# Rows of x stored from GpSimd's queue instead of SyncE's, and expert 0's first weights requested two iterations earlier

## The chip, the cores and the metric

One core of one Trainium2 chip runs the whole program. Its engines are TensorE (PE, with its weight loads shown as PEld), VectorE (DVE), ScalarE (ACT), GpSimd (POOL) and SyncE (SP); here SP only issues transfers. The metric is the device time of one execution in microseconds (us); lower is better.

## The reference, cut to what matters

Local attention over chunks of 64 positions is followed by a mixture of eight experts, all in fp32. B=8, S=576, eight heads of 64, F=1024.

```python
scores = scale * q_c @ k_c.T                  # per chunk of 64, scale = 1/8
attn = softmax(scores);  x = attn @ v_c       # x: [B, S, 512] after the heads are joined
for b in range(B):
    prev_e = -1
    for s in range(S):
        fresh_e = argmax(x[b, s] @ w_gate)
        e = fresh_e if s == 0 or sigmoid(x[b, s] @ w_local) < 0.5 else prev_e
        prev_e = e
        out[b, s] = softmax(x[b, s] @ w_gate)[e] * (relu(x[b, s] @ w1[e]) @ w2[e])
```

## The kernel before, in words

**Attention.** The 4608 rows are cut into 18 units of 256 rows. `place` maps a unit to its rows: sixteen units are 256 neighbouring rows of one batch; units 4 and 13 are leftover units, made of the last 64 rows of each of four batches. A unit goes through these steps: `load_qk` and `load_v` bring q, k and v in; `a_pair` (`pair_heads`, line 174) has POOL copy q and k into the buffers `qr` and `kr`, two copies each; `a_tq` transposes these on PE, and ACT moves the result out of PSUM; `a_sa` makes scores and their softmax; `a_tp` transposes the probabilities; `a_va` makes the values and writes normalised rows to `xs`; `a_tx` transposes these; `a_ra` (`router`) makes the gate's logits, copies them beside the rows (line 320, `xs<-L`) and stores rows and logits in the DRAM tile `x_d`. An `xs` tile is 128 partitions of two rows of 528 floats, 528 KB in all.

**Software pipeline.** Fifteen iterations of the loop at line 848 play the order `PAR["steady"]`, each working on several units at once: iteration i loads q and k of unit i+5 and v of unit i+2, runs scores of unit i+1, probabilities of unit i, values of unit i-1, transposes of q and k of unit i+2, and router and store of unit i-2, and at its end the POOL copies of unit i+3. The `qr` and `kr` buffers exist once, so these copies wait until PE has read the ones before. q and k have three load buffers each, v three, `xs` four. Order on PE, ACT, DVE and POOL is the order of the program (`manual_schedule`); every queue works in order, so an instruction that waits holds what is behind it.

**Weights of expert 0.** `load_w1(0, c)` requests a quarter of the first weight matrix (512 KB) into `raw1[c]`, after iterations 6, 8, 10 and 12. After iterations 8 to 15 `split` turns half a quarter into a high part (ACT, line 105, `w1h`) and a low part (POOL, line 106, `w1l`): quarter c is split after iterations 8+2c and 9+2c.

**Routing and experts.** `PAR["hooks"]` places the routing of the first nine units (`route`, `slots`) into iterations 10 to 15: small chains over DVE and PE, one-hot rows `rh` on DVE and POOL (line 464, in iteration 14), and `early_gather`, three indirect transfers on POOL's queue that read `x_d` (line 673). After the loop `PAR["drain"]` finishes the last four units beside the first expert tiles; then tiles of 128 rows go through their experts, with gathers and scatters on POOL's queue.

**Queues.** SP issues every plain transfer: q, k, v, weights, and the rows of x. POOL issues only the indirect ones.

Of the kernel before, what the change touches and what calls it, by code (L numbers as in the profile page):

```python
# [20 lines left out]
B, H, S, D = 8, 8, 576, 64  # L21
# [3 lines left out]
P = 128  # L25
# [49 lines left out]
def tile_attention_then_moe(ctx: ExitStack, tc, q, k, v, wg, wl, w1, w2, out):  # L75
    nc = tc.nc
# [5 lines left out]
    x_d = dpool.tile([N, XR], F32, name="x_d")  # L82
# [15 lines left out]
    def load_w1(e, c):  # L98
        nc.sync.dma_start(raw1[c], w1[e, P * c:P * c + P, :])

    def load_w2(e, c):
        nc.sync.dma_start(raw2[c], w2[e, 256 * c:256 * c + 256, :].rearrange("(f p) d -> p f d", p=P))

    def split(hi, lo, raw, lo_eng=None):
        nc.scalar.copy(hi, raw)
        (lo_eng or nc.vector).tensor_tensor(lo, raw, hi.bitcast(F32), ALU.subtract)
# [20 lines left out]
    def place(i):  # L127
        ph, j = divmod(i, 9)
        if j == LEFT:
            return 9 * ph + 8, [(4 * ph + n, 512, 64) for n in range(4)]  # L130
        j -= j > LEFT
        return 9 * ph + j, [(4 * ph + j // 2, 256 * (j % 2), 256)]
# [163 lines left out]
    def router(i, xT, xs, fine=False):  # L296
        lg = ps_l.tile([P, 2, 256], F32, name="lg")
        lT = pa2.tile([P, LW], F32, name="lT", bufs=1)[:, 0:256]

        def mm():  # L300
            for c in range(4):
                nc.tensor.matmul(lg[32 * c:32 * c + 32, 0], wg9[:, c], xT[:, c], start=True, stop=True)
            if not fine:
                cp()

        def cp():
            nc.vector.tensor_copy(lT, lg[:, 0])

        def tr():
            for cc in range(2):  # L310
                nc.tensor.transpose(lg[:, 1, P * cc:P * cc + P], lT[:, P * cc:P * cc + P], ident)
            if not fine:
                red()

        def red():
            slot, rows = place(i)
            Lt = L[:, 2 * slot:2 * slot + 2, :]
            nc.vector.tensor_reduce(
                Lt, lg[:, 1].rearrange("p (t c e) -> p t e c", t=2, c=4)[:, :, 0:9, :], AX.X, ALU.add)
            nc.vector.tensor_copy(xs[:, :, C:XL], Lt)  # L320
            if len(rows) == 1:
                (b, s0, n), = rows
                nc.sync.dma_start(x_d[S * b + s0:S * b + s0 + n, :].rearrange("(c p) n -> p c n", p=P), xs)
            else:
                for m, (b, s0, n) in enumerate(rows):
                    nc.sync.dma_start(x_d[S * b + s0:S * b + s0 + n, :], xs[64 * (m // 2):64 * (m // 2) + 64, m % 2])

        return [mm, cp, tr, red] if fine else [mm, tr]

    def ok(i):  # L330
        return 0 <= i < NS
# [140 lines left out]
    def a_tq(i, engs=None):  # L472
        qkT[i] = (pe2.tile([P, 4, 256], F32, name="qT", bufs=1), pe2.tile([P, 4, 256], F32, name="kT", bufs=1))
        return qk_transposes(hd.pop(i), *qkT[i], engs)

    def a_pair(i, engs=(nc.gpsimd,) * 4):
        hd[i], fns = pair_heads(qk.pop(i), engs)
        return fns

    def a_sa(i, fine=False):  # L480
        prs[i] = pa2.tile([P, H, 2, D], F32, name="pr")
        return scores(*qkT.pop(i), prs[i], fine)

    def a_tp(i, fine=False):
        pTs[i] = pa2.tile([P, H, P], F32, name="pT")
        return p_transposes(prs.pop(i), pTs[i], fine)

    rows = []

    def a_va(i, fine=False):  # L490
        if not rows:
            rows.extend(pa2.tile([P, XS], F32, name=f"xs{n}", bufs=1) for n in range(NX))
        xss[i] = rows[i % NX][:, 0:2 * XR].rearrange("p (c n) -> p c n", c=2)
        if i < NX:
            nc.gpsimd.memset(xss[i][:, :, XL:XR], 0.0)
        return values(pTs.pop(i), vts.pop(i), xss[i], fine)

    def a_tx(i, fine=False):
        xTs[i] = pa2.tile([P, 4, 256], F32, name="xT", bufs=1)
        return x_transposes(xss[i], xTs[i], fine)  # L500

    def a_ra(i, fine=False):
        return router(i, xTs.pop(i), xss.pop(i), fine)

    def play(order, qs):
        its = {}
        for tok in order.split():
            name, _, n = tok.partition("*")
            if name not in its:
                its[name] = iter(qs[name]())  # L510
            for _ in range(int(n or 1)):
                next(its[name])()
        for name, it in its.items():
            assert next(it, None) is None, name
        assert set(its) == set(qs), set(qs) - set(its)

    def run(fns):
        for fn in fns:
            fn()
# [54 lines left out]
    with tc.manual_schedule(engines=MAN | {ET.Pool}):  # L574
# [3 lines left out]
        def load(store, fn, i):  # L578
            def go():
                store[i] = fn(i)  # L580
            return lambda: [go]
# [266 lines left out]
    for i in range(1, NS - 2):  # L848
        qs4 = dict(s=lambda: a_sa(i + 1), tp=lambda: a_tp(i), va=lambda: a_va(i - 1, True), tq=lambda: a_tq(i + 2))
        opt = dict(lq=load(qk, load_qk, i + 5) if ok(i + 5) else None,  # L850
                   lv=load(vts, load_v, i + 2) if ok(i + 2) else None,
                   pr=(lambda: a_pair(i + 3)) if ok(i + 3) else None, tx=(lambda: a_tx(i - 2)) if i >= 2 else None, ra=(lambda: a_ra(i - 2, True)) if i >= 2 else None)
        for h in range(4):
            opt[f"h{h}"] = (lambda h=h: [lambda: run(hooks[i, h])]) if (i, h) in hooks else None
        toks = [t for t in PAR["steady"].split() if opt.get(t.split("*")[0], 1) is not None]
        play(" ".join(toks), qs4 | {k: v for k, v in opt.items() if v is not None})
        if i in (6, 8, 10, 12):
            load_w1(0, i // 2 - 3)
        if 8 <= i < 16:
            c, col = divmod(i - 8, 2)  # L860
            col = slice(512 * col, 512 * col + 512)
            split(w1h[c][:, col], w1l[c][:, col], raw1[c][:, col], nc.gpsimd)
# [9 lines left out]
    n = NS - 1  # L872
# [27 lines left out]
    def gather_full(t):  # L900
        xgs[t] = gather(t, pc.tile([P, XR], F32, name="xg", bufs=4), x_d)
# [27 lines left out]
        s=lambda: sa, ld=lambda: [lambda: [load_w2(0, c) for c in (2, 3)]], rt=lambda: sb, rk=sb_rank, of=lambda: offsets, oh=sb_onehots,  # L929
        sl=lambda: slots([pc, pc, pc], QB[1], QB[2], ((0, NT),), qs), ex=lambda: experts,  # L930
        g=lambda: [lambda t=t: gather_full(t) for t in (EARLY, EARLY + 1)],
# [294 lines left out]
```

## Time and profile before

| | |
|---|---|
| time, median of 3 runs | 650.72 us (648.82 to 650.81) |
| profiled execution, its own time | 656.88 us |
| its span, first to last instruction | 655.1 us |
| mean granted clock of TensorE over the span | 0.991 |
| PE busy | 616.1 us, 94% of the span |
| DVE, ACT, POOL busy | 378.2, 258.2, 147.2 us |
| attention with its router | about the first 172 us |

Times inside the trace count from the start of the span. In the rows, an arrow from the right ("out<-in") names what an instruction writes and reads, "xN" counts instructions merged in one row, and square brackets hold the idle time of the engine just before the row and what ended it. A row "SPq" is SP issuing a transfer; its length is the time that SP needed to hand it over, not the time to its landing. A busy PE is not PE at its peak.

### The profile page before, as it was taken

The numbers are of one execution on the slowest core, as the hardware profiler recorded it, in microseconds if no ns is written. First come the engines' busy times: TensorE is split into PE (matmuls) and PEld (weight loads), VectorE is DVE, ScalarE is ACT, GpSimd is POOL, SyncE is SP. The second block draws the span as 40 slices with busy tenths as digits, with TensorE's granted clock in tenths as the row PEclk, the third lists the DMA queues.
The fourth block names the chain that finished last, engine by engine and source line by source line (L and its number), as shares of the span: only waits on it lengthen the run. The fifth ranks groups of instructions, "written<-read, shape, count | busy, mean of one in ns | idle before, by whom it ended". The sixth has DMA issues, their size and how long they took to land. (4 is left out here: it accounts for less than half of the span.)

```text
span 655.1 us, 17357 instructions
## 1 busy us (share of the span) xinstructions
PE 616.1 (94%) x5904; PEld 517.2 (79%) x5904; DVE 378.2 (58%) x983; ACT 258.2 (39%) x469; POOL 147.2 (22%) x217
## 2 busy tenths in 40 slices
PE   4799997989999999999999999999998999999995
PEld 4678886766788788788899996789887988788883
DVE  2567676987784767475433465763477533377231
ACT  4567785756412153531212433531464211343130
POOL 4423343550050112022021021022011212010201
PEclk9999998999999999999999999999998999999998
DMA  8999899989622054055121065451075511154201
GB/s 241 237 275 292 229 267 288 294 218 310 197 77 94 35 181 170 28 179 175 39 68 52 22 212 157 146 173 56 33 246 209 189 53 49 37 180 134 82 21 37
DMA packets 102521, 97.90 MB, mean 149 GB/s; under 512 B 42256, under 2 KB 79120, under 8 KB 102352
## 3 DMA queue, kind: packets, MB, share of 16 engines
q1 hardware_dynamic: 96192, 75.82, 38.7%
q0 software_dynamic: 6160, 19.99, 9.3%
q8 instruction: 86, 1.41, 0.9%
q14 instruction: 83, 0.68, 0.4%
HBM read 76.62 MB, written 19.69 MB: 147 GB/s over the span
## 5 line engine op out<-in xcount | busy, mean ns | idle before, releaser
L783 POOL DMA_INDIRECT out<-ysb,sidx x38 | 40.9, 1076 | 364.4 <-DVEq L979 163.2
L722 PE MATMUL y<-w2h,hq 128*128 128x512 f32 x368 | 119.4, 395 | 1.2 <-ACTq L1001 1.0
L1014 PEld LDWEIGHTS tr<-xp,w1h 128*128 128x128 f32 x704 | 87.7, 191 | 4.0 <-ACT w2h L963 1.5
L1014 PE MATMUL tr<-xp,w1h 128*128 128x256 f32 x704 | 90.2, 283 | 0.7 <-ACTq L979 0.5
L722 PEld LDWEIGHTS y<-w2h,hq 128*128 128x128 f32 x368 | 69.3, 189 | 16.7 <-issue 2.1
L722 PE MATMUL y<-w2l,hq 128*128 128x512 f32 x184 | 72.2, 393 | 2.5 <-DVE w2l L969 1.5
L1022 ACT ACTIVATE hq<-tr 128x256 fp32r<-128x256 f32 x68 | 25.2, 383 | 107.4 <-PE tr L1014 60.9
L722 PE MATMUL y<-w2h,hp 128*128 128x512 f32 x192 | 63.1, 396 | 0.5 <-ACT hp L669 0.3
L701 PE MATMUL h<-w1h,xp 128*128 128x512 f32 x208 | 60.8, 398 | 0.0
L1023 DVE SCALAR_TENSOR_TENSOR hq<-tr,hq 128x256 fp32r<-128x256 f32 x68 | 28.1, 424 | 38.7 <-ACT hq L1022 36.8
L1014 PE MATMUL tr<-xp,w1l 128*128 128x256 f32 x352 | 47.6, 283 | 0.0
L1014 PEld LDWEIGHTS tr<-xp,w1l 128*128 128x128 f32 x352 | 44.6, 192 | 0.0
L701 PEld LDWEIGHTS h<-w1h,xp 128*128 128x128 f32 x208 | 37.8, 188 | 7.6 <-ACTq L979 0.4
L722 PEld LDWEIGHTS y<-w2l,hq 128*128 128x128 f32 x184 | 34.8, 189 | 10.2 <-DVE w2l L969 2.4
L673 POOL DMA_INDIRECT xg<-x_d,gidx x36 | 38.3, 1064 | 19.5 <-issue 13.3
L722 PEld LDWEIGHTS y<-w2h,hp 128*128 128x128 f32 x192 | 36.0, 188 | 8.3 <-DVE hp L670 0.6
L768 ACT ACTIVATE hsb<-h 128x512 f32<-128x512 f32 x26 | 14.1, 596 | 65.6 <-PE h L701 49.4
L969 DVE TENSOR_TENSOR w1l<-raw,w1h 128x1024 fp32r<-128x1024 f32 x28 | 32.4, 1220 | 12.1 <-ACT w1h L963 10.6
L722 PE MATMUL y<-w2l,hp 128*128 128x512 f32 x96 | 37.6, 392 | 0.5 <-DVE w2l L969 0.5
L1043 DVE TENSOR_SCALAR ysb<-y,ppr 128x512 f32<-128x512 f32 x32 | 24.0, 751 | 23.5 <-PE y L722 22.5
L969 DVE TENSOR_TENSOR w2l<-raw,w2h 128x1024 fp32r<-128x1024 f32 x28 | 32.8, 1221 | 5.2 <-ACT w2h L963 3.2
L963 ACT CAST w2h<-raw 128x1024 fp32r<-128x1024 f32 x28 | 28.0, 1046 | 13.8 <-PE m L734 3.8
(229 smaller groups left out, 1062.3 us busy)
## 6 DMA issues: line engine op xcount, KB each, us to landing
raw<-in_moe_w SPq DMA_DIRECT2D x72, 512.0 KB
x_d<-xs SPq DMA_DIRECT2D x16, 528.0 KB
qt<-in_q SPq DMA_DIRECT2D x15, 512.0 KB
kt<-in_k SPq DMA_DIRECT2D x15, 512.0 KB
v<-in_v SPq DMA_DIRECT2D x20, 256.0 KB
raw<-in_v SPq DMA_DIRECT2D x12, 256.0 KB
x_d<-xs SPq DMA_DIRECT2D x8, 132.0 KB
qt<-in_q SPq DMA_DIRECT2D x8, 128.0 KB
```

The source lines that it names most:

```text
L673: nc.gpsimd.indirect_dma_start(out=dst, out_offset=None, in_=src, in_offset=bass.IndirectOffsetOnAxis(ap=gidx[t].bitcast(U32), axis=0))
L701: nc.tensor.matmul(hs[:, j], xs[a][:, c], W1[w][c][:, 512 * j:512 * j + 512], start=(c == 0 and n == 0), stop=(c == 3 and n == 2))
L722: nc.tensor.matmul(y, h_of(t, f // 4)[a][:, f % 4], W2[w][c][:, f % 2, :], start=(f == 0 and n == 0), stop=(f == 7 and n == 2))
L768: nc.scalar.activation(hsb[:, 512 * j:512 * j + 512], hs[:, j], AF.Relu)
L783: nc.gpsimd.indirect_dma_start(out=out, out_offset=bass.IndirectOffsetOnAxis(ap=sidx[t].bitcast(U32), axis=0), in_=ysb, in_offset=None, bo ...
L963: nc.scalar.copy(hi[c], raw[c])
L969: V.tensor_tensor(lo[c], raw[c], hi[c].bitcast(F32), ALU.subtract)
L1014: nc.tensor.matmul(hb[:, 256 * n:256 * n + 256], W1[w][c][:, P * (f + n):P * (f + n) + P], XP[:, x, c].rearrange("p s t -> p (s t)"), star ...
L1022: nc.scalar.activation(hi, ps, AF.Relu)
L1023: V.scalar_tensor_tensor(lo, ps, 0.0, hi.bitcast(F32), ALU.max, ALU.subtract)
L1043: V.tensor_scalar(ysb, y, pr, None, ALU.mult)
```

## The change

The rows of a unit go to `x_d` from POOL's queue, with the same shape as before for an ordinary unit; a leftover unit's four stores of 64 rows become two of 128 rows. The requests for expert 0's first weights move from the end of iterations 6, 8, 10, 12 to the end of 4, 6, 8, 10; their splits stay.

```diff
             nc.vector.tensor_copy(xs[:, :, C:XL], Lt)
+            xv = x_d.rearrange("(b s) n -> b s n", s=S)
             if len(rows) == 1:
                 (b, s0, n), = rows
-                nc.sync.dma_start(x_d[S * b + s0:S * b + s0 + n, :].rearrange("(c p) n -> p c n", p=P), xs)
+                nc.gpsimd.dma_start(xv[b, s0:s0 + n].rearrange("(c p) n -> p c n", p=P), xs)
             else:
-                for m, (b, s0, n) in enumerate(rows):
-                    nc.sync.dma_start(x_d[S * b + s0:S * b + s0 + n, :], xs[64 * (m // 2):64 * (m // 2) + 64, m % 2])
+                for g in range(2):
+                    b, s0, n = rows[2 * g]
+                    nc.gpsimd.dma_start(xv[b:b + 2, s0:s0 + n].rearrange("c p n -> p c n"), xs[64 * g:64 * g + 64])
...
-        if i in (6, 8, 10, 12):
-            load_w1(0, i // 2 - 3)
+        if i in (4, 6, 8, 10):
+            load_w1(0, i // 2 - 2)
```

## Rows read from the trace of the kernel before

**Rows 1.** Windows: stretch, length, busy us (count) per engine, clock, DMA share, GB/s.

```profile
60.50:67.80 7.30, 7.30 (x173) 5.95 (x172) 5.24 (x15) 5.48 (x10) 2.34 (x4) 1.00 1.07 287
...
75.00:82.20 7.20, 7.20 (x171) 5.94 (x170) 5.13 (x14) 5.39 (x10) 2.34 (x4) 1.00 0.71 197
96.80:109.70 12.90, 9.50 (x178) 7.49 (x176) 8.06 (x27) 7.50 (x14) 4.27 (x7) 0.87 1.04 292
...
134.50:143.20 8.70, 7.92 (x189) 6.57 (x188) 6.73 (x24) 5.57 (x10) 4.03 (x5) 1.00 0.57 166
...
200.00:420.00 220.00, 217.09 (x1318) 185.74 (x1316) 124.81 (x309) 69.81 (x134) 34.78 (x33) 1.00 0.34 111
```

**Rows 2.** Timeline of SP's queue, 64 to 144 us, some of its rows.

```profile
64.94 1.84 SPq L323 DMA_DIRECT2D x_d<-xs  x1
...
73.49 4.88 SPq L326 DMA_DIRECT2D x_d<-xs  x4
78.41 0.58 SPq L99 DMA_DIRECT2D raw<-in_moe_w  x1
...
95.03 0.46 SPq L99 DMA_DIRECT2D raw<-in_moe_w  x1
...
102.91 1.32 SPq L323 DMA_DIRECT2D x_d<-xs  x1
...
115.12 5.03 SPq L154 DMA_DIRECT2D v<-in_v  x4
...
134.96 2.31 SPq L323 DMA_DIRECT2D x_d<-xs  x1
143.07 1.62 SPq L154 DMA_DIRECT2D v<-in_v  x2
```

**Rows 3.** Timeline, all engines, around the split of the second quarter.

```profile
101.47 0.62 ACT L105 CAST w1h<-raw 128x512 fp32r<-128x512 f32 x1 [2.91 <-DMA raw<-in_moe_w]
...
102.72 0.63 PE L182 MATMUL tr<-ident,qr 128*128 128x128 f32 x4 [2.46 <-ACT xT L172]
...
109.35 0.49 PE L388 MATMUL tr<-ident,sc 18*1 18x18 f32 x4 [0.84 <-DVE sc L381]
```

**Rows 4.** Windows of 5 us around that wait, columns as in rows 1.

```profile
45.00:50.00 5.00, 3.42 (x86) 2.82 (x80) 2.62 (x6) 2.48 (x5) 0.00 (x0) 1.00 1.02 309
...
100.00:105.00 5.00, 2.54 (x21) 1.68 (x20) 3.00 (x7) 2.90 (x6) 2.44 (x3) 0.89 1.05 283
105.00:110.00 5.00, 4.06 (x65) 3.22 (x66) 2.10 (x9) 3.15 (x5) 1.17 (x2) 0.77 1.06 296
```

**Rows 5.** Timeline of iteration 6 and the start of iteration 7.

```profile
60.57 1.16 PE L211 MATMUL sc<-kT,qT 64*64 64x64 f32 x64
...
64.53 1.17 POOL L174 COPY qr<-qt 128x512 f32<-128x512 f32 x2 [4.46 <-issue]
...
67.79 1.16 PE L211 MATMUL sc<-kT,qT 64*64 64x64 f32 x64
...
68.02 0.18 DVE L320 COPY xs<-L 128x18 f32<-128x18 f32 x1
...
70.54 1.09 PE L182 MATMUL tr<-ident,qr 128*128 128x128 f32 x8
```

**Rows 6.** Line 673, POOL's indirect transfers: instructions (ns min/median/max), and two in the timeline.

```profile
L673 POOL DMA_INDIRECT xg<-x_d,gidx x36: 944/979/1952, 191.9 to 618.1; - x36
...
143.21 0.96 POOL L673 DMA_INDIRECT raw<-x_d,gidx  x1 [0.31 <-issue]
...
144.47 0.95 POOL L673 DMA_INDIRECT raw<-x_d,gidx  x1 [0.30 <-issue]
```

**Rows 7.** Timeline of iterations 14 and 15.

```profile
126.77 0.69 PE L260 MATMUL o<-v,pT 64*64 64x65 f32 x31
...
128.40 5.39 POOL L464 TENSOR_SCALAR rh<-iota_m,rq 128x128 bf16<-128x128 bf16 x9
...
134.73 0.20 DVE L320 COPY xs<-L 128x18 f32<-128x18 f32 x1
...
138.34 1.09 PE L182 MATMUL tr<-ident,qr 128*128 128x128 f32 x8
```

## The prediction, made before the change was run

> **What bounds the kernel now.** I read the windows first, then SP's queue, then the places where PE stands still, then POOL's place in one iteration. In iteration 6 PE has no gap: 7.30 us busy in 7.30, and from its scores to the next iteration's it is 67.79 - 60.57 = 7.22 us [rows 1, 5]. So in plain iterations PE sets the pace. The DMA engines, though, are as full: their share is 1.07 there, and 1.04 from 96.8 to 109.7 [rows 1]. SP's queue shows what that does. The rows of unit 4, complete near 68.2 [rows 5], are handed over only at 73.49, and the quarter of w1 requested after iteration 6 only at 78.41, that after iteration 8 at 95.03 [rows 2]. The queue runs more than an iteration late, and it is empty again at 134.96, where a store leaves 0.03 us after its rows were ready [rows 2, 7]. Stores, loads and weights share one order, so the late thing that hurts is whichever is needed soonest.
>
> That is the second quarter of w1. ACT waits 2.91 us for it at the end of iteration 10, and PE, behind ACT, stands 2.46 us [rows 3]. Then the granted clock is 0.89 and 0.77 in the two windows that follow (a mean of the levels 2.4 and 1.2 GHz); a shorter rest, 1.58 us between 45 and 50, left it at 1.00 [rows 4]. Afterwards PE is the bound again: from 200 to 420 it is busy 217.09 of 220 us with a DMA share of 0.34 [rows 1]. Nothing there can take up or hide a change in the length of attention, so what attention gains or loses, the end gains or loses.
>
> **The change, part by part.** *Weights two iterations earlier.* The four requests are the same four; each is merely two iterations, some 14.4 us, sooner in SP's order. The second quarter would then leave near 95.03 - 14.4 = 80.6 and is wanted at 101.47 - 2.91 = 98.56 [rows 2, 3]: even 5 us later it is in time. The removed wait gives 2.46 us [rows 3]. The clock's dip gives (1 - 0.89) x 5 + (1 - 0.77) x 5 = 1.70 us [rows 4]; from below it gives nothing, if the dip comes without the rest, but a rest stood before it, so I take it whole: -4.2 us. The 0.84 us in which PE waits for a routing scan stays [rows 3]. The third quarter needs the same shift: 4.2 us sooner in PE's time its old place would be too late.
>
> *Stores off SP's queue.* SP hands over nothing that PE waits for directly except loads; a store took 1.32 to 2.31 us of SP's time and the leftover unit's four took 4.88, with the DMA share down to 0.71 from 75.0 to 82.2 [rows 1, 2]. That hand-over time is hidden now behind full DMA engines: I count it at nothing. The bytes stay the same, 528 KB a unit, so full engines gain nothing either. But POOL's stores now leave when the rows are ready, ahead of loads in front of which they did not stand before. A store is 0.54 MB; at 287 GB/s that is 1.9 us, and a quarter of w1 1.8 us [rows 1]. A load therefore has one quarter and about one store more in front of it than today, 3.7 us, less (1 - 0.71) x 7.2 = 2.1 us if the idle share is used up [rows 1]: 1.6 us. The tightest load I see is v of unit 13: it is handed over by 115.12 + 5.03 = 120.15 and first multiplied at 126.77 [rows 2, 7]. Of these 6.6 us PE, 4.2 sooner, leaves 2.4; less 1.6 that is 0.8 us in which it must land. The cover is just about gone there: I count 0 in the sum and 2.5 us as the bound.
>
> *Stores on POOL's queue.* Here is the new wait. In program order a store stands ahead of the four POOL copies of its iteration. Today the copy of q starts at 64.53, when PE has freed the buffer; then it must stand behind rows ready at 68.02 + 0.18 = 68.20. The copied q is wanted by PE at 70.54 [rows 5]. One copy takes 1.17 / 2 = 0.59 us. Leaving 0.1 us for signals, POOL may spend 70.54 - 68.20 - 0.59 - 0.1 = 1.65 us on a store before PE waits; everything above is paid in each iteration, as the copies, the transposes and the next router form a ring. No direct transfer of POOL's is in this trace. The nearest row is its indirect one of 128 rows: 0.96 us and 0.30 us ahead of it, 1.26 [rows 6]. Lower bound: 0.944 and no lead. Upper bound: cost by the row, 256 rows for 128, 2 x 1.26 = 2.52 us. I take 1.26, since an indirect transfer also has to read an index for every row and a direct one does not: no wait in the ordinary iterations. At 2.52 us, eleven iterations (2 to 13 but the leftover one) lose 0.87 each, +9.6 us.
>
> The leftover store in iteration 6 is two transfers, 2.52 us: 2.52 - 1.65 = +0.9 us, met by PE in iteration 7. The second leftover store, in iteration 15, has no copies behind it. In iteration 14 the store also stands ahead of the last third of the one-hot rows: nine take 5.39 us, so three 1.8 [rows 7]. Then rows at 134.93, store to 136.2, one-hot rows to 138.0, first copy to 138.6, against 138.34 where PE wants it: +0.4 us with the second copy. Splits and early gathers behind stores have microseconds to spare: the split's result is first used after the loop.
>
> The longest of POOL's indirect transfers took 1.952 us against a median of 0.979 [rows 6]; with the lead that would be 2.25, 0.6 over the room, +7 us over eleven iterations and iteration 14. The Trainium skill, page "SBUF — State Buffer", section "SBUF: two separate sides", says that a transfer issued from GpSimd waits for its descriptors while VectorE runs in a two-port mode, and advises SP or ACT as issuer. By that rule the stores would sit at the long end; the median row speaks against it, as VectorE was at work beside those transfers too.
>
> *Sum*, against the profiled execution (656.88 us, span 655.1): -2.46 - 1.70 + 0.9 + 0.4 = -2.9 us. The timed runs are 6 us shorter (650.72), so waits in them may be smaller; I carry the sum over as it is: 650.7 - 2.9 = 647.8 us.
>
> **Rivals.** *The gain is not there to be had.* Either the timed runs, 6 us shorter than the profiled one, hold no wait for w1, or the loads that the stores overtake take its place. For it: DMA shares above 1 in rows 1 and the 2.4 us left to v of unit 13. Against it: the waiting quarter is 2.91 us late, and the third would follow [rows 3]. Without a wait the sum is +1.3, about 652.0; with the wait gone and 2.5 us of late loads it is -0.4, about 650.3. I put the case at 650.7, no change. The Trainium skill, page "DMA: Bandwidth & Descriptors", section "Issuing engines are not separate DMA queues", says that transfers of all issuers interleave on the same 16 engines and only issue time is saved by spreading them. By that rule half of this rival holds: the stores' move buys loads nothing.
>
> *POOL becomes the ring's bound: slower.* One mechanism: a store of 256 rows takes POOL more than 1.65 us [rows 5, 6]. At 1.95 us it costs 0.3 x 12 = 3.6, and the sum is +0.7; at 2.52 it is 9.6 + 0.9 more in iteration 14 - 2.9 = +7.6, about 658.3. It turns the sign at about 1.9 us (0.24 x 12 = 2.9). I price it at 2.2 us: 0.55 x 12 - 2.9 = +3.7, 654.4. For it: the store has twice the gather's rows. Against it: the index.
>
> *The change doesn't do what it says*: excluded for the weights, whose buffers are free from the start; the stores are plain transfers.
>
> **How the numbers follow.** Forecast case 0.47, no gain 0.31, POOL's ring 0.22. About 0.3% (2 us) is what a measurement here can tell from no change. Of the forecast case 0.41 lies beyond 2 us and 0.06 within; of no gain 0.02 faster, 0.26 same, 0.03 slower; of the ring 0.02, 0.03, 0.17. That makes faster 0.45, same 0.35, slower 0.20. The forecast case reaches from 645.5 (no wait in iterations 7 and 14, and 1 us less of the rest between 45 and 50 [rows 4]) to 650.0; the range takes in no gain and half of the ring's case: 645.0 to 653.5.
>
> **What would show it.** ACT no longer waits for the weights at the end of iteration 10, and no window near 105 has a clock below 1. POOL shows a store right after `xs<-L` and the q copy right behind, with PE's q transposes unmoved in ordinary iterations and late by about 0.9 in iteration 7. Wrong would be: stores of over 1.65 us on POOL with PE waiting for `qr` in every iteration; PE waiting for v or q; or an attention that ends sooner while the whole does not.

## The result, and the profile after

The changed kernel takes 658.24 us (median of 4 runs, 655.58 to 660.25) against 650.76 us for the kernel before (4 runs, 648.82 to 651.86). The ratio is 1.0108, with a 95% interval of 1.0078 to 1.0138: 1.1% slower, where 647.8 us had been forecast. The profiled execution took 660.13 us (span 658.2, clock 0.987), against 656.88 (span 655.1, clock 0.991).

What the change was to do to the weights and to GpSimd's queue is in the trace. First the two groups of stores, line by line (count, shortest, median and longest time in ns, first and last start):

```profile
L324 POOL DMA_DIRECT2D x_d<-xs x16: 725/732/987, 37.3 to 175.0; - x16
...
L328 POOL DMA_DIRECT2D x_d<-xs x4: 603/634/673, 68.2 to 152.2; - x4
```

A store of 256 rows holds GpSimd for 0.73 us, less than the indirect transfer of half the rows [rows 6], and far from the 1.65 us of room. The timeline of iterations 6 and 7 shows the order that follows:

```profile
59.83 0.72 POOL L324 DMA_DIRECT2D x_d<-xs  x1 [4.23 <-DVE xs L320]
60.56 1.17 POOL L174 COPY qr<-qt 128x512 f32<-128x512 f32 x2
...
61.67 1.16 POOL L174 COPY kr<-kt 128x512 f32<-128x512 f32 x2
...
63.04 1.09 PE L182 MATMUL tr<-ident,qr 128*128 128x128 f32 x8
...
68.22 1.21 POOL L328 DMA_DIRECT2D x_d<-xs  x2 [5.39 <-DVE xs L320]
69.43 1.17 POOL L174 COPY qr<-qt 128x512 f32<-128x512 f32 x2
...
70.84 0.34 PE L211 MATMUL sc<-kT,qT 64*64 64x64 f32 x8 [2.41 <-issue]
```

GpSimd waits for `xs<-L`, stores, and only then copies q and k. The q copies are done at 61.7, 1.3 us before PE transposes them, and in the whole of attention after 30 us PE never waits for `qr` (once, for 0.41 us, for `kr`). But the copies have moved, from the middle of an iteration (64.53, some 3.5 us ahead of `xs<-L`, in [rows 5]) to behind that instruction, into the start of the next one. PE's wait of 2.41 us has no releaser that the profile shows ("issue"); it stands in the middle of a group of score matmuls.

The wait for w1 has gone. The split that waited 2.91 us [rows 3] now has no bracket, since the last of the four quarters was requested at 84.51:

```profile
104.45 0.62 ACT L105 CAST w1h<-raw 128x512 fp32r<-128x512 f32 x1
```

Iteration 11, counted between the starts of two `xs<-L`, fell from 11.59 to 8.74 us. Iteration 14 is where the other sign is plainest. Its timeline, to be read against [rows 7]:

```profile
129.58 0.73 POOL L324 DMA_DIRECT2D x_d<-xs  x1 [4.03 <-DVE m L456]
...
130.31 1.18 POOL L174 COPY qr<-qt 128x512 f32<-128x512 f32 x2
130.31 1.76 DVE L459 CAST ri<-rk 128x18 int32<-128x18 f32 x1
...
131.42 1.17 POOL L174 COPY kr<-kt 128x512 f32<-128x512 f32 x2
...
132.11 1.76 DVE L460 TENSOR_SCALAR ri<-ri 128x18 int32<-128x18 int32 x1
132.56 1.27 POOL L106 TENSOR_TENSOR w1l<-raw,w1h 128x512 fp32r<-128x512 f32 x1
...
138.50 0.29 PE L260 MATMUL o<-v,pT 64*64 64x65 f32 x4 [3.85 <-DVE xs L274]
```

The same two VectorE instructions in the kernel before, and what follows them, from its timeline:

```profile
126.67 0.18 DVE L457 CAST ri<-rk 128x18 int32<-128x18 f32 x1
126.88 0.18 DVE L458 TENSOR_SCALAR ri<-ri 128x18 int32<-128x18 int32 x1
...
126.94 1.31 POOL L106 TENSOR_TENSOR w1l<-raw,w1h 128x512 fp32r<-128x512 f32 x1 [2.72 <-ACT w1h L105]
...
127.17 1.13 DVE L460 CAST rq<-ri 128x36 f32<-128x36 int32 x1
```

Two routing instructions of 18 columns take 1.76 us each instead of 0.18, and each ends within 0.1 us of the end of a GpSimd instruction. The kernel before is not free of this either: there one cast (L460) took 1.13 us beside GpSimd's half of a split, and in the changed kernel that cast takes 0.18 us. So VectorE loses 2 x 1.58 - 0.95 = 2.2 us more than before. It works in order, the scores' maximum and `xs` stand behind these instructions, and PE waits 3.85 us for `xs` (1.14 in the kernel before). The iteration takes 11.48 us instead of 9.26, which is 2.2 us longer. Windows of the changed kernel, with the columns of [rows 1], show what follows on the clock:

```profile
67.00:74.00 7.00, 4.59 (x106) 3.89 (x108) 3.37 (x7) 3.20 (x5) 3.48 (x6) 0.81 1.08 308
...
140.00:145.00 5.00, 5.00 (x113) 4.31 (x112) 4.10 (x16) 3.71 (x6) 3.90 (x7) 0.69 0.76 216
...
200.00:420.00 220.00, 216.28 (x1316) 184.92 (x1315) 124.50 (x306) 70.59 (x135) 35.41 (x35) 1.00 0.34 112
```

After the rest in iteration 14 the granted clock is 0.69 over 5 us, a loss of (1 - 0.69) x 5 = 1.6 us; round the rest in iteration 7 it is 0.81 over 7 us. From 200 to 420 next to nothing has changed against [rows 1]. The last `xs<-L` starts at 174.52 us against 171.03, and what follows it takes 484 us in both traces: the loss lies in attention.

### The profile page after: what moved, and what is told of

It reads as the page before. It is cut to its first block, busy times and chain, and to the rows that moved or that the text cites. A ratio compares the mean times of both kernels' runs of the same rounds, so it can differ in the third digit from the quotient of the medians.

```text
span 658.2 us, 17346 instructions
## 1 busy us (share of the span) xinstructions
PE 617.5 (94%) x5904; PEld 519.1 (79%) x5904; DVE 380.1 (58%) x983; ACT 257.6 (39%) x469; POOL 161.3 (25%) x237
## 5 line engine op out<-in xcount | busy, mean ns | idle before, releaser
L703 PE MATMUL h<-w1h,xp 128*128 128x512 f32 x208 | 60.8, 398 | 0.0
L222 DVE TENSOR_REDUCE mx<-sc 128x8 f32<-128x512 f32 x36 | 23.1, 684 | 20.0 <-PE sc L211 20.0
```

The source lines that it names most:

```text
L222: nc.vector.tensor_reduce(mxs[a], sc.rearrange("p j h c k -> p (j h c) k")[:, a:b], AX.X, ALU.max)
L703: nc.tensor.matmul(hs[:, j], xs[a][:, c], W1[w][c][:, 512 * j:512 * j + 512], start=(c == 0 and n == 0), stop=(c == 3 and n == 2))
```

## The experiments

Three theories were on record for the first runs. A: SP's order. SP's queue is ordered by a planner, not by the program; with the stores gone it draws the weights forward, ahead of loads. B: the place of the stores on GpSimd, which makes its copies late. C: the transfers in a ring of their own (GpSimd's instead of SP's), where they take the DMA engines' time earlier than before. Later runs divide B into B1 (the late copies meet VectorE's routing) and B2 (they cost time in the iterations before it), and add D (SP, without the stores' waits, runs ahead). Every ratio is to the kernel before on the same chip (20 to 28 runs of it, median 652.3 to 655.6 us).

**Weights alone.** The kernel before, with only

```diff
-        if i in (6, 8, 10, 12):
-            load_w1(0, i // 2 - 3)
+        if i in (4, 6, 8, 10):
+            load_w1(0, i // 2 - 2)
```

> The kernel before with the first expert's w1 requested after iterations 4, 6, 8 and 10, and nothing else; the stores stay on SP. If the loss of 7.5 us comes from the stores' move (own ring, POOL's order, or the loads that it lets the scheduler pull forward on SP), this one is 647 to 651 us, not slower than before. If the earlier weights themselves push q, k and v back, it is slower, 653 us or more.

Measured: 0.9986 (0.9969 to 1.0004). In the trace the wait for w1 is gone and the span is 650.5 us, 4.6 less; but that execution was the shortest of its ten, and the timed runs together leave a gain of 2 us at most. So the stores cause the loss, and most of the gain was one of the profiled executions.

**SP in program order.** The changed kernel, with SP's queue in the order of the program:

```diff
-    man = tc.manual_schedule(engines=MAN | {ET.Pool})
+    man = tc.manual_schedule(engines=MAN | {ET.Pool, ET.SP})
```

> The changed kernel with SP's queue in the order of the program through the loop and the drain, so that w1's quarters stay behind iterations 4, 6, 8, 10 and w2's first two behind the last v. Theory A (the loss is in SP's order: weights handed over ahead of v): back to 649 to 652 us. Theory B (the POOL copies that now run later and meet VectorE's routing) and theory C (stores in a ring of their own take DMA time from loads and from instruction fetches): no better than the changed kernel, 655 to 660 us.

Measured: 1.0115 (1.0079 to 1.0150), as slow as the changed kernel. Theory A falls.

**Store behind the copies.** The changed kernel, each store issued behind the four copies of its iteration (two runs: SP's queue as planned, and in program order):

```diff
+            held.append(lambda: store(xs, rows))      # in red()
...
+        run(held)                                     # behind play(...)
+        held.clear()
```

> The changed kernel with each store in the loop issued behind POOL's four copies of its iteration instead of ahead of them, so that the copies run where they ran before; stores stay on POOL. Theory B: VectorE's two slow conversions in iteration 14 (1.76 us each) are gone, PE's wait of 3.85 us falls to about 1.1, and the time falls by 2 to 4 us, to about 654. Theories A and C: no change beyond 1 us.

> Both edits together: program order on SP and the store behind the copies. If A and B are both right and add up, 647 to 650 us, at or below the kernel before; if C holds, still 653 us or more.

Measured: 1.0020 (0.9993 to 1.0048) and 1.0023 (0.9991 to 1.0055). GpSimd still issues every store; only its place among the copies is another, and the loss is nearly gone. That fits theory B, and C as the whole cause falls. But the edit moves two things at once: the copies come earlier, and the stores later.

**Which stores.** The changed kernel again, with the stores late in some iterations only (`held` for units 0 to 7; for unit 11; for units 8 to 13), and the changed kernel itself a second time:

> The changed kernel with the stores of units 0 to 7 (iterations 2 to 9) issued behind GpSimd's four copies, those of units 8 to 13 where the change put them. Theory B1 (the stores ahead of the copies cost time only where the routing runs, iterations 10 to 15): as slow as the changed kernel, ratio to before 1.008 to 1.012, iteration 14 at 11.5 us. Theory B2 (they cost it in the iterations before the routing, above all in 6 and 7, round the leftover unit): ratio 1.002 to 1.005, iterations 6 and 7 at 7.2 to 8.3 us each.

> The changed kernel with only the store of unit 11 (iteration 13) behind GpSimd's copies, so that the copies of iteration 13 are done before VectorE's routing instructions of iteration 14. Theory B1: iteration 14 falls from 11.5 to about 9.4 us, the wait of 3.85 us on PE goes back to about 1.1, and the ratio to before falls from 1.011 to 1.005 to 1.008; if this meeting is the whole loss, to 1.002. Theory B2: ratio stays at 1.009 to 1.012.

> The changed kernel itself once more, beside the others on one chip. Both theories: ratio to before 1.008 to 1.014; iterations 6, 7 and 14 show whether 8.6, 11.5 and 11.5 us come again.

> The changed kernel with the stores of units 8 to 13 (iterations 10 to 15) behind GpSimd's copies and those of units 0 to 7 where the change put them. If the meeting with the routing is the loss: ratio 1.001 to 1.004, as with all stores late, iterations 11 to 14 at 7.5, 9.2, 7.5 and 9.4 us. If the early stores cost time before the routing: 1.005 to 1.009.

Measured: units 0 to 7 late 1.0080 (1.0051 to 1.0109); unit 11 late 1.0065 (1.0039 to 1.0090); changed kernel again 1.0111 (1.0074 to 1.0148); units 8 to 13 late 1.0022 (0.9992 to 1.0052). The stores of iterations 10 to 15, where the routing runs, carry about 0.9 of the 1.1% (give or take 0.4). The timeline of the last of these kernels in iteration 14:

```profile
123.89 0.73 POOL L332 DMA_DIRECT2D x_d<-xs  x1 [1.71 <-DVE m L464]
...
124.61 0.18 DVE L467 CAST ri<-rk 128x18 int32<-128x18 f32 x1
...
124.82 0.18 DVE L468 TENSOR_SCALAR ri<-ri 128x18 int32<-128x18 int32 x1
124.90 1.30 POOL L106 TENSOR_TENSOR w1l<-raw,w1h 128x512 fp32r<-128x512 f32 x1 [0.28 <-ACT w1h L105]
```

The store is there, the copies are over (120.94 + 1.24 = 122.18 us), and the two instructions are back at 0.18 us, as in the kernel before. Iteration 11 shows the same meeting on a smaller scale, in the changed kernel:

```profile
103.12 0.74 POOL L324 DMA_DIRECT2D x_d<-xs  x1 [4.55 <-DVE mxb L359]
...
103.47 0.67 DVE L361 TENSOR_TENSOR t<-t,idxm 128x144 f32<-128x144 f32 x1
...
104.07 0.58 DVE L366 SCALAR_TENSOR_TENSOR ab<-L,notfirst 128x18 f32<-128x18 f32 x1
...
105.24 0.53 DVE L369 TENSOR_TENSOR ab<-mxb,ab 128x18 f32<-128x18 f32 x1
```

and with units 8 to 13 late:

```profile
99.96 0.31 DVE L369 TENSOR_TENSOR t<-t,idxm 128x144 f32<-128x144 f32 x1
...
100.19 0.18 DVE L374 SCALAR_TENSOR_TENSOR ab<-L,notfirst 128x18 f32<-128x18 f32 x1
...
100.85 0.18 DVE L377 TENSOR_TENSOR ab<-mxb,ab 128x18 f32<-128x18 f32 x1
```

**The meeting from its other side.** The changed kernel with the routing moved and the stores left alone; and the kernel before with one store alone on GpSimd:

```diff
-    ... 54, 55, 55, 56, 57, 58, ...
+    ... 54, 57, 57, 57, 57, 58, ...                   # PAR["hooks"]
```

> The changed kernel with the end of VectorE's routing of batch group 0 (L459 to L462, L829 to L831) one place later in iteration 14, behind its score work, so that it does not meet GpSimd's copies. Theory B1 (the meeting in iteration 14 costs 0.3 to 0.5%, as the late store of unit 11 showed): iteration 14 at 9.3 to 9.9 us, these instructions at 0.2 us each, ratio 1.005 to 1.008. If the meeting is not the cause: 1.009 to 1.013.

```diff
-                nc.sync.dma_start(
+                (nc.gpsimd if i == 11 else nc.sync).dma_start(
```

> The kernel before with the store of unit 11 alone on GpSimd's queue, ahead of the copies. Theory B1: iteration 14 at 11.5 us and ratio 1.003 to 1.006. If only all stores together cost the time: ratio 0.999 to 1.002, iteration 14 at 9.3 us.

Measured: 1.0065 (1.0041 to 1.0089), the two instructions at 0.17 us, though iteration 14 still takes 10.57 (VectorE now stands still in it, and PE rests 1.8 us with no releaser shown); and 1.0071 (1.0042 to 1.0100), iteration 14 at 11.94. One store out of eighteen, in the one iteration where VectorE routes beside the copies, makes the old kernel 0.7% slower, a little more than was expected. Its timeline:

```profile
122.53 0.98 POOL L323 DMA_DIRECT2D x_d<-xs  x1 [5.56 <-DVE m L455]
...
123.25 3.79 DVE L458 CAST ri<-rk 128x18 int32<-128x18 f32 x1
...
123.50 1.18 POOL L174 COPY qr<-qt 128x512 f32<-128x512 f32 x2
...
124.61 1.17 POOL L174 COPY kr<-kt 128x512 f32<-128x512 f32 x2
...
125.75 1.26 POOL L106 TENSOR_TENSOR w1l<-raw,w1h 128x512 fp32r<-128x512 f32 x1
```

One cast of 18 columns starts at 123.25 and ends at 127.04, with the last of five GpSimd instructions that follow one another without a gap (125.75 + 1.26 = 127.01).

**Late copies without the stores.** The kernel before, stores on SP, with one or three small GpSimd copies where the change has the store:

```diff
+            if fine:
+                for n in range(3):                    # one copy in the first of the two runs
+                    nc.gpsimd.tensor_copy(gapc[:, 2 * n:2 * n + 2], xs[:, :, C])
```

> The kernel before with one small GpSimd copy (128x2) in the place of the new store: it waits on the same VectorE instruction, so GpSimd's four copies come as late as in the changed kernel, while the stores stay on SP and the w1 requests where they were. Theory B (the late copies cost the time, not the transfer): ratio 1.006 to 1.011, iteration 14 at about 11.5 us. Theory C (the stores in GpSimd's own ring cost it, by their transfers or by what SP pulls forward): ratio 0.999 to 1.003, iteration 14 at 9.3 us.

> The kernel before with three small GpSimd copies (128x2, 0.23 us each) in the place of the new store, so that GpSimd is held about as long as by the store's 0.73 us and its four copies lie where they lie in the changed kernel. Theory B (where the copies lie decides): iteration 14 at 11.5 us, not 10.6 as with one small copy, and ratio 1.003 to 1.006. Theory C (the stores outside SP's queue): ratio 0.999 to 1.003.

Measured: 1.0013 (0.9996 to 1.0030) and 1.0032 (1.0010 to 1.0055), with iteration 14 at 10.62 and 11.07 us. The three copies took 0.59 us, not 0.73, so the alignment is not quite the changed kernel's. Late copies lengthen iteration 14 with no store on GpSimd at all. But the ratio is at most a third of the whole loss, less than theory B alone called for, and the first of the two cannot be told from none. So theory C stays possible for a part of the loss: a part may belong to the transfers that leave early in a ring of their own.

What the meeting does to iteration 14 can be read from VectorE's starts in six traces. In none of the six does the timeline mark a gap of VectorE there, so the iteration is as long as its work. The first stretch, from `xs<-L` to the maximum of the scores (line 222), holds the routing; the second goes on to the next `xs<-L`. Times in us:

| kernel | with the routing | rest | iteration 14 |
|---|---|---|---|
| before | 3.12 | 6.14 | 9.26 |
| units 8 to 13 late | 3.12 | 6.13 | 9.25 |
| before, one small copy | 4.41 | 6.21 | 10.62 |
| before, three small copies | 4.68 | 6.39 | 11.07 |
| changed | 5.35 | 6.13 | 11.48 |
| before, unit 11 on GpSimd | 5.80 | 6.14 | 11.94 |

The time that VectorE loses in its routing is, but for 0.25 us, the time by which the iteration grows.

**SP's waits.** The changed kernel, with a transfer of 36 bytes on SP where each store of iterations 2 to 15 was:

```diff
+            if fine:
+                nc.sync.dma_start(t_d[i:i + 1, 0:9], xs[0:1, 0, C:XL])
```

> The changed kernel with one small transfer (1x9 of xs, 36 bytes) on SP in the place of each store of iterations 2 to 15, so that SP waits for xs there as before and requests loads and weights in the order and at the pace of before, while the rows are stored from GpSimd. Theory D (SP, without the stores' waits, requests loads earlier and in bursts, and PE's instruction fetches come late): iterations 3 to 10 together at 58 to 60 us, not 64 to 66, and ratio 1.005 to 1.008. Theory B or C without D: ratio 1.009 to 1.013.

Measured: 1.0066 (1.0031 to 1.0101), inside what theory D had called for; but iterations 3 to 10 took 65.4 us in its trace, not 58 to 60, and the interval reaches that of the changed kernel. Inconclusive.

**Stores before the routing.** The kernel before with the stores of units 0 to 10, then of units 0 to 7, on GpSimd's queue and all others on SP:

```diff
+            q = nc.gpsimd if i < 11 else nc.sync      # i < 8 in the last run
```

> The kernel before with the stores of units 0 to 10 on GpSimd's queue ahead of the copies, those of unit 11 and later on SP, so that the meeting of iteration 14 cannot happen. If the early stores cost what the meeting leaves unexplained (1.011 less 0.005): ratio 1.004 to 1.008, iterations 3 to 10 together above 61 us, iteration 14 at 9.4 us. If nearly all of the loss is the meeting: ratio 0.999 to 1.002, iterations 3 to 10 at 58 to 60 us.

> The first of these four once more, since the effect looked for is about as large as the interval of one run. Both theories as there; the two ratios should lie within 0.004 of each other.

> As the run before it, with the stores of units 0 to 10 issued behind GpSimd's four copies. If the late copies cost the time in the early iterations: ratio 0.999 to 1.002. If the transfers in a ring of their own, or SP without its waits, cost it: the same ratio as with the early stores, 1.004 to 1.008.

> As the first of these runs, with a transfer of 1x9 of xs on SP in the place of each of these stores, so that SP keeps its waits. If SP without its waits costs the time (loads requested earlier, PE's instruction fetches late): ratio 0.999 to 1.002. If the late copies or the transfers cost it: 1.004 to 1.008.

> The kernel before with the stores of units 0 to 7 (iterations 2 to 9) on GpSimd's queue ahead of the copies and all later ones on SP: GpSimd's copies come late only where VectorE has no routing to do. If the loss comes from VectorE's routing instructions meeting the late copies (iterations 11, 13 and 14): ratio 1.000 to 1.004, iterations 11 to 14 at 7.5, 9.2, 7.5 and 9.4 us but for waits on weights. If the early stores cost time in the iterations before the routing too: 1.005 to 1.009.

Measured: units 0 to 10 early 1.0094 (1.0065 to 1.0122) and 1.0070 (1.0047 to 1.0093); late 1.0030 (1.0002 to 1.0058); early, with SP's waits kept, 1.0105 (1.0068 to 1.0142); units 0 to 7 early 1.0063 (1.0040 to 1.0086). All of these carry the change's form of the leftover stores, and the weights at their old place. Theory D falls here: with SP's waits the loss is as large. The last run is a miss for "the meeting is everything": its routing in iteration 14 is clean (8.33 us, not even a split meets it) and it is 0.6% slower all the same. Its windows and its waits of PE before the routing:

```profile
37.00:95.00 58.00, 53.30 (x1237) 43.29 (x1229) 36.57 (x92) 39.93 (x67) 24.87 (x42) 1.00 1.02 286
...
PE sc L211 <- issue: 3.5, 4, 1.6
PE o L260 <- issue: 0.7, 1, 0.7
PE tr L182 <- issue: 0.3, 1, 0.3
```

against the window of the kernel with the weights alone changed, where PE has no gap:

```profile
37.00:95.00 58.00, 58.00 (x1366) 47.60 (x1364) 41.51 (x106) 44.31 (x75) 19.54 (x32) 1.00 1.02 270
```

The kernels side by side; times are differences between starts of `xs<-L` in each trace, in us:

| kernel | iterations 3 to 10 | 11 | 13 | 14 | ratio |
|---|---|---|---|---|---|
| before | 59.8 | 11.59 | 7.56 | 9.26 | 1 |
| weights alone | 57.8 | 9.20 | 7.54 | 9.44 | 0.9986 |
| changed | 65.8 | 8.74 | 8.27 | 11.48 | 1.0108 |
| changed, again | 64.0 | 8.75 | 7.48 | 11.86 | 1.0111 |
| all stores late | 61.7 | 7.53 | 7.53 | 9.43 | 1.0020 |
| all stores late, SP in program order | 63.8 | 9.26 | 7.61 | 9.43 | 1.0023 |
| units 8 to 13 late | 62.4 | 7.52 | 7.53 | 9.25 | 1.0022 |
| units 0 to 7 late | 60.8 | 8.69 | 7.48 | 11.41 | 1.0080 |
| unit 11 late | 63.5 | 8.75 | 8.62 | 9.92 | 1.0065 |
| before, unit 11 on GpSimd | 59.6 | 7.52 | 7.89 | 11.94 | 1.0071 |
| before, units 0 to 7 on GpSimd | 64.3 | 8.84 | 8.16 | 8.33 | 1.0063 |
| before, units 0 to 10 on GpSimd | 62.2 | 8.75 | 8.61 | 9.24 | 1.0094 |
| the same, again | 63.1 | 8.75 | 8.62 | 9.81 | 1.0070 |
| before, units 0 to 10 on GpSimd, late | 63.0 | 7.53 | 8.06 | 9.43 | 1.0030 |

One trace is one execution: the two of the same kernel with units 0 to 10 on GpSimd have spans of 653.6 and 658.5 us, so a difference of a microsecond or two between single traces shows little.

## Why the prediction was wrong

**The step that failed** is "Stores on POOL's queue. Here is the new wait", with the sentence that closes it, "no wait in the ordinary iterations". It asked one question of the late copies: do they still reach PE in time? They do. The price of 1.26 us for a store was too high (0.73 measured), the two of a leftover unit cost 1.21 us and not 2.52, and neither the +0.9 us of iteration 7 nor the +0.4 us of iteration 14 came about through `qr`. What the step did not ask is which engine the copies run beside at their new place. They start with VectorE's routing of iterations 11 and 14, and VectorE's instructions there last until GpSimd's are over. Against the kernel before, that is 2.2 us more of VectorE in iteration 14, and against the one with all stores late 0.36 + 0.40 + 0.35 = 1.1 us in iteration 11; the iterations grew by 2.2 and 1.2 us. Taking the meeting of iteration 14 away by either of its sides gives back about 0.45%; putting the stores of all iterations with routing behind the copies gives back 0.9%; making the meeting of iteration 14 in the old kernel costs 0.7%. For iteration 14 the cause is shown; it does not carry the whole loss.

The Trainium skill has this rule on the page from which the prediction took another: "SBUF — State Buffer", section "SBUF: two separate sides", says that VectorE and GpSimd share a pair of ports that one of them holds for a whole instruction while the other stands still, and that VectorE wants it for its fast modes and for two inputs from SBUF. The trace agrees: the instructions held are casts, scalar operations and operations on two SBUF inputs (1.76 us instead of 0.18, 0.67 instead of 0.31), while the reductions beside them keep their time (0.29 and 0.30). The prediction used only the sentence on descriptors, in the direction from VectorE to GpSimd; here hardly a store was held up (0.73 us in the median, at most 0.99).

**Weights two iterations earlier.** The mechanism was right: no wait for w1 is left, and iteration 11 is shorter. Its worth was mis-sized: -4.2 us in the sum, 4.6 us in the profiled pair, but 0.9986 (0.9969 to 1.0004) in timed runs. The rival "the gain is not there to be had" had named the reason: the timed runs may hold no such wait. The traces bear it out. The kernel with unit 11's store on GpSimd differs from the kernel before only by that store, in iteration 13; yet in its trace the same split in iteration 10 does not wait, and iteration 11 takes 7.52 us:

```profile
98.98 0.62 ACT L105 CAST w1h<-raw 128x512 fp32r<-128x512 f32 x1
```

In the two traces with small copies, whose stores and weights are also where they were before, the split waits 0 and 1.21 us. So the 2.91 us belong to one execution, and the prediction took them for the kernel's. The rival's other half, loads that become late, showed nowhere: PE did not wait for v of unit 13. Also, "merely two iterations sooner in SP's order" held for the weights alone (requests at 58.6, 77.3, 94.2 and 109.8 us, from 78.4 to 128.3 before); with the stores gone from SP as well, the planner drew the four together, from 58.3 to 84.5.

**GpSimd as the ring's bound.** The rival of the right sign gave 658.3 us at its upper bound and the measurement is 658.24, but by another mechanism: a store is far below 1.65 us, and PE does not wait for `qr`. That agreement is chance.

**"Splits and early gathers behind stores have microseconds to spare"** held.

**What stays open.** The parts do not add up. Units 0 to 7 on GpSimd cost 0.6% with the other stores on SP and the weights at their old place, but nothing that can be measured when the later stores are on GpSimd too, behind the copies, and the weights are early (1.0022 against 1.0020 with all late); no run changed only one of the two. In the traces every kernel with these stores on GpSimd ahead of the copies takes 62 to 66 us for iterations 3 to 10, those with them behind the copies 61 to 64, those with them on SP 58 to 61. So the copies' place cannot be all of it. What is added are rests of PE in the middle of groups with no releaser shown: between 36 and 102 us, those of 0.4 us and more add up to 3.0 to 5.9 us a trace with the stores ahead of the copies, 1.6 to 4.8 behind them, and 0 to 1.6 on SP.

The traces point to a reason that no run tested. One of the DMA queues that the profile calls "instruction" (q8) moves a packet of 16 KB about every 6 us. Between 36 and 140 us the twenty traces have 79 such rests, and 78 of them end 2.1 to 2.9 us after one of these packets starts; the DMA engines are full there (a share of 1.08 in the window from 67 to 74). That fits instructions for PE that come late when stores leave early, which would be a form of theory C; it is argued, not shown.

How timed runs make 3 to 5 us of 2 us in iteration 14 is not shown either. Some of it even comes back: from the `xs<-L` that ends it to the last one it is 33.9 us in the changed kernel, 36.3 before and 37.1 with units 8 to 13 late. Part of the rest is the clock. The median of the timed runs' mean granted clock falls from 0.991 to 0.988 with the changed kernel again, from 0.9925 to 0.990 with unit 11 alone and from 0.989 to 0.984 with units 0 to 7; as a share of the time, an estimate, that is 2.0, 1.6 and 3.3 us of 8.3, 4.0 and 4.6. No version beat the kernel before by more than its interval; the weights alone come nearest.

## What to carry to other kernels

A transfer that is put on a computing engine's queue brings its wait along, and in an in-order queue everything behind it moves to the moment when that wait ends. So ask not only whether the moved work is still in time for its reader, but beside which instructions of other engines it will then run; here a store of 0.73 us did much of its harm by moving copies onto VectorE's routing. Issue such a store behind the work that does not need its data. And do not book a wait seen in one profiled execution as a gain: look for it in a second one first, above all when the timed runs are shorter than the first by more than the wait.

## What was not expected of the hardware

A VectorE instruction that meets GpSimd does not merely wait for the current instruction's end: a cast of 128x18 took 3.79 us, as long as the rest of an unbroken row of five GpSimd instructions, where it takes 0.18 us alone. In other runs such instructions got in between two of GpSimd's, after 0.27 to 1.88 us. And a direct store of 256 rows (528 KB) costs GpSimd 0.73 us, one of 128 rows 0.60 to 0.67, less than an indirect transfer of 128 rows (0.98).
